# Block 0's convolution with two product buffers, a split of its last taps between GpSimd and VectorE, and carried rows loaded in pieces

## The chip, the cores and the metric

The program runs on one core of one Trainium2 chip. The engines that matter are TensorE (PE in the rows; PEld is its weight load), VectorE (DVE), ScalarE (ACT), GpSimd (POOL), and SyncE (SP), whose queue issues the transfers. The metric is the device time of one execution in microseconds; less is better. A kernel's time is the median of several executions.

## What is computed

A dynamic convolution over 7 positions, with softmax weights, feeds two fully connected pairs.

```python
B, S, D = 2, 4096, 192            # H, K = 8 heads, 7 taps; group = D // H = 24
w = exp(weight_gen - max(weight_gen, axis=-1)); w = w / (sum(w, axis=-1) + 1e-09)
x_pad = concatenate([zeros((B, K - 1, D)), x], axis=1)
out[b, s, h, :] = sum over k of w[b, s, h, k] * x_pad[b, s + k, h, :]
x = out.reshape(B * S, D)                                    # 8192 tokens
h = x @ moe_w_in                                             # 192 -> 2048
x = where(h >= 1, h, where(h <= -1, 0, (h + 1) ** 2 / 4)) @ moe_w_out
h = x @ moe2_w_in
return (h - tanh(h)) @ moe2_w_out                            # 8192 x 192, float32
```

## The kernel before

**Tiling.** Each of the 128 partitions holds 64 consecutive tokens of one sequence. The 8192 tokens are worked in 16 blocks `b` of 512, four tokens (`T`) of every partition. A block passes its convolution (`conv`), its first pair (`m = 0`) and its second pair (`m = 1`). A pair takes 16 items of 128 hidden columns: five matmuls into a bank (`mm1`, L540), the activation (L546 to L548, or L550 and L551), a split of the result into a rounded part `gh` (L552) and a rest `gl` (L556), and the second matmuls (L564 to L571, or L581 to L584).

**Weights.** Both pairs' weights arrive as 64-bit words in chunks (`weights`): ScalarE and VectorE join the halves (L305, L310, L314, L319), ScalarE casts the high part (L337), and VectorE or GpSimd makes the low part (L341). All 32 chunks are prepared in the first 180 us or so.

**The convolution of an early block (0 and 1).** `load_wg` (L375) brings the softmax weights' inputs, `load_halo` the carried rows: the first taps of a partition's first tokens need up to six rows of the partition before it, `w[lo+1:hi, 0:n0]`, 63 partitions for each of the two sequences, in two transfers (L386); the one partition without a neighbour is set to zero by GpSimd (L385). `load_x` (L378) brings the rest. The softmax is L406 to L416; its result `wg` is copied to PSUM (L427), so that VectorE can read it there. VectorE multiplies four taps (L419), each into the one product area `prod_ps` in PSUM, and adds each to `acc` (L461). GpSimd multiplies the other three into `taps`, in SBUF, and adds them up (L445). `last_sum` adds the two partial sums in two pieces, L468 to `acc` and L470 into `xw`; both inputs are in SBUF. Then TensorE transposes (L478, L481), and ScalarE and VectorE split the result (L498 to L510) for the first `mm1`.

**The order of the work.** `Plan` builds each engine's order ahead of time: every task has an engine or a choice of engines, a duration, a key and the slots that it takes. `run` steps through time and gives a free engine its ready task of lowest key. For VectorE it models a lock: a task marked `lock` waits while GpSimd works, and its key grows by that wait. Chunk weights with the lowest key go ahead of convolution steps with a higher one; block 0's convolution has keys from -60, block 1's from `CONV1`. The transfers are issued from SP's queue in the planned order, and wait there for their buffers.

Of the kernel before, what the change touches and what calls it, by code (L numbers as in the profile page):

```python
# [17 lines left out]
P = 128  # L18
N = 512
T = N // P  # L20
LAG = 3
RAW = 4
EARLY = 2
POOL_TAPS = (3, 3)
REBIAS = 2.0 ** -112
ITEM = 2.275

# [19 lines left out]
class Plan:  # L47
# [20 lines left out]
    def run(self):  # L68
# [17 lines left out]
        while events:  # L86
# [10 lines left out]
            for e in ready:  # L97
                if free[e] > now + 1e-9:
                    continue
                kept, got = [], None  # L100
                pool_busy = max(0.0, free.get("POOL", 0.0) - now) if e == "DVE" else 0.0
                if pool_busy:

                    ready[e] = [(t.key + t.engines[e][1] + (pool_busy / ITEM if t.lock else 0.0), t.order, t) for _, _, t in ready[e] if t.start is None]
                    heapq.heapify(ready[e])
                while ready[e]:
                    c = heapq.heappop(ready[e])
                    t = c[2]
                    if t.start is not None:
                        continue  # L110
                    pick, ok = [], True
                    for s in t.takes:
                        n = s.choice()
                        if n is None:
                            ok = False
                            break
                        s.free.remove(n)
                        pick.append((s, n))
                    if ok:
                        for s, n in pick:  # L120
                            s.n = n
                        got = t
                        break
                    for s, n in reversed(pick):
                        s.free.insert(0, n)
                    kept.append(c)
                for c in kept:
                    heapq.heappush(ready[e], c)
                if got is None:
                    continue  # L130
                t, dur = got, got.engines[e][0]
                if e == "DVE" and t.lock:
                    dur += pool_busy
                    free["POOL"] = max(free.get("POOL", 0.0), now + dur)
                    locked = now + dur
                elif e == "POOL" and locked > now:
                    dur += locked - now
                t.start, t.engine, t.took = now, e, dur
                t.seen = now + dur + t.late
                free[e] = now + dur  # L140
                heapq.heappush(events, now + dur)
                heapq.heappush(events, t.seen)
                done.append(t)
                for s in t.uses:
                    s.users -= 1
                    if s.users == 0:
                        heapq.heappush(returns, (t.seen, t.order, id(s), s))
                for d in t.next:
                    d.blocked -= 1
                    if d.blocked == 0:  # L150
                        when = max(q.seen - (q.late - q.own if q.engine in d.engines else 0.0) for q in d.deps)
                        heapq.heappush(waiting, (when, d.order, d))
                        heapq.heappush(events, when)
# [9 lines left out]
def tile_dynconv_moe_moe(  # L163
# [43 lines left out]
    make_identity(nc, ident)  # L207
    half = const.tile([P, 1], F32, tag="half", name="half")
    nc.vector.memset(half, 0.5)

    nc.scalar.activation(const.tile([P, 1], F32, tag="warm", name="warm"), half, AF.Exp)


    win = tiles("win", 2, [P, 4, FF], F32R)
    wout = tiles("wout", 2, [P, NF, 2 * D], F32R)
# [144 lines left out]
    def conv(b, banks, base, gap):  # L360
# [15 lines left out]

        def load_x(e):
            e.dma_start(xws[xw.n][:, n0:, :], x_pj[:, j0 - PAD + n0:j0 + T, :])  # L378

        def load_halo(e):  # L380

            w = xws[xw.n]
            for q in range(B):
                lo, hi = q * BP, (q + 1) * BP
                nc.gpsimd.memset(w[lo:lo + 1, 0:n0, :], 0.0)  # L385
                e.dma_start(w[lo + 1:hi, 0:n0, :], x_pj[lo:hi - 1, J - n0:J, :])  # L386

        def bc(t):
            return t.unsqueeze(3).to_broadcast([P, T, H, K])
# [35 lines left out]

        if early:
            tw = plan.add(on("ACT", 0.30), key(), lambda e: e.copy(wg_ps, W()), [ts], uses=[wg] + area)  # L427
            mine = K - POOL_TAPS[b]
            prod, wsrc = prod_ps, lambda: wg_ps
            dep = [tw]  # L430

            def pool_mem(k):
                return xt_t[spare.n][:, k]

            pt = [ts, lx, lh]
            first = True
            for k in range(mine, K):
                def ptap(e, k=k, first=first):
                    if first:
                        xt_tile(spare, f"taps{b}", (P, 2, T, D), F32)  # L440
                    tap(e, pool_mem(0 if first else 1), W(), k)

                pt = [plan.add(on("POOL", 1.6), base, ptap, pt, takes=[spare] if first else [], uses=[wg, xw] + ([] if first else [spare]), late=0.1)]
                if not first:
                    pt = [plan.add(on("POOL", 1.6), base, lambda e: e.tensor_tensor(pool_mem(0), pool_mem(0), pool_mem(1), op=ALU.add), pt, uses=[spare], late=0.1)]  # L445
                first = False
            addend = lambda: pool_mem(0)
        else:
            mine = K
            prod, wsrc = prod_sb, W  # L450
            dep, pt = [ts], []
            addend = lambda: prod_sb
        more = (area if early else [])
        for k in range(mine):
            def mult(e, k=k):
                tap(e, prod if k else acc_sb, wsrc(), k)

            t = plan.add(on("DVE", 0.87), key(), mult, dep + [whole(k), lh], takes=[] if k else [mem], uses=[wg, xw] + more + ([mem] if k else []), late=0.1, own=0.12 if early and k else 0.0, lock=not early)
            dep = [t]
            if k and (k < mine - 1 or early):  # L460
                t = plan.add(on("DVE", 0.87), key(), lambda e: e.tensor_tensor(acc_sb, acc_sb, prod, op=ALU.add), dep, uses=[mem] + more, late=0.1, lock=not early)  # L461
                dep = [t]

        flat = lambda: xws[xw.n].rearrange("p j d -> p (j d)")[:, 0:T * D1]

        def last_sum(e):
            s = addend()
            e.tensor_tensor(acc_sb[:, :, 0:P], acc_sb[:, :, 0:P], s[:, :, 0:P], op=ALU.add)  # L468

            e.tensor_tensor(flat().rearrange("p (t c) -> p t c", t=T), acc_sb[:, :, P:D], s[:, :, P:D], op=ALU.add)  # L470

        t = plan.add(on("DVE", 0.97), key(), last_sum, dep + pt, uses=[mem, xw] + more + ([spare] if early else []), lock=True)

        p0, p1 = ps[banks[0]], ps[banks[1]]

        def transposes(e):
# [6 lines left out]
        last = key()  # L483
        tr = plan.add(
            on("PE", 0.70), last, transposes, [t, marks.get(("fin1", 0 if b == 2 else b - 1)) if b == 2 or b > 3 else None],
            takes=[] if early else area, uses=[mem, xw] + more, late=0.4,
        )
        X = lambda k: xt_t[xt.n][:, k]

# [166 lines left out]
UNTIL = 3.5  # L656
SKEW = 12
LEAD = (4.0, 6.0)
CONV1 = (4.0, 0.35)
CONV2 = (14.0, 0.6)  # L660


# [27 lines left out]
```

## Time and profile before

| | us |
|---|---|
| median of 3 runs (1232.03 to 1232.91) | 1232.22 |
| the profiled execution | 1232.54 |
| its span, first to last instruction | 1230.7 |
| TensorE busy in the span | 1193.1 |
| VectorE busy | 984.5 |
| ScalarE busy | 831.5 |
| GpSimd busy | 100.2 |

The profiled execution has 1.84 us around its span. A row of the timeline is one instruction or some alike: start, duration, engine, line, operation, names, and in brackets how long the engine had been idle and what ended that. Two instructions of VectorE that depend on each other follow with a small gap; two that don't may overlap by a little.

### The profile page before, as it was taken

What the parts mean: (1) busy time and instruction counts of PE and PEld (TensorE: products, weight loads), DVE (VectorE), ACT (ScalarE), POOL (GpSimd) and SP (SyncE); (2) the same over time, 40 slices, a digit from 0 to 9 for tenths busy, and PEclk for the clock granted to TensorE, in tenths of its full rate; (3) what the DMA queues carried; (4) which work ended last, traced back from release to release, by engine and by line L of the source; (5) the groups of instructions that cost most, each with busy time, mean ns of one, the idle gap of its engine ahead of it and who ended that gap; (6) DMA issues with size and microseconds to landing.
All of it is one profiled execution on the core that took longest, in us unless ns stands there. A gap on an engine that the chain in (4) does not pass through costs nothing.

```text
span 1230.7 us, 16226 instructions
## 1 busy us (share of the span) xinstructions
PE 1193.1 (97%) x5984; PEld 1024.9 (83%) x5984; DVE 984.5 (80%) x1535; ACT 831.5 (68%) x1500; POOL 100.2 (8%) x84
## 2 busy tenths in 40 slices
PE   3799999999999999999999999999999999999998
PEld 2577879889888898988889888888988889888897
DVE  7999988868779697886968779696887968676665
ACT  5888985675766657576675766667576675766654
POOL 5644560000000000000000000000000000000000
PEclk9899999999999999999999999999999999999999
DMA  8422221001000010100101000010100000000000
GB/s 218 141 88 67 72 77 45 18 1 32 18 32 18 1 36 14 33 17 4 46 1 33 18 32 17 1 37 14 33 17 18 29 1 1 13 1 14 1 14 13
DMA packets 16494, 39.55 MB, mean 32 GB/s; under 512 B 1828, under 2 KB 8098, under 8 KB 16416
## 3 DMA queue, kind: packets, MB, share of 16 engines
q1 hardware_dynamic: 16416, 38.53, 9.9%
q8 instruction: 46, 0.75, 0.3%
q14 instruction: 32, 0.26, 0.1%
HBM read 32.23 MB, written 6.29 MB: 31 GB/s over the span
## 4 chain that ended last, share of the span: by engine, by line
PE 85%; DVE 0%; DVEq 0%; issue 0%
PE ps L540 43%; PE ps L581 14%; PE ps L582 7%; PE ps L565 4%; PE ps L564 4%; PE ps L566 4%; PE ps L571 4%; PE ps L570 4%; PE ps L584 1%; PE ps L478 0%; PE ps L481 0%; DVE raw L618 0%; DVE ps L314 0%; DVE g L551 0%; DVEq L686 0%
## 5 line engine op out<-in xcount | busy, mean ns | idle before, releaser
L556 DVE TENSOR_TENSOR gl<-g,gh 128x512 fp32r<-128x512 f32 x475 | 329.6, 696 | 184.8 <-ACT gh L552 182.1
L552 ACT CAST gh<-g 128x512 fp32r<-128x512 f32 x512 | 315.6, 617 | 202.9 <-DVE g L551 182.5
L540 PE MATMUL ps<-a,win 128*128 128x512 f32 x1280 | 340.8, 397 | 8.2 <-DVE g L548 6.9
L540 PE MATMUL ps<-b,win 128*128 128x512 f32 x1280 | 339.2, 395 | 1.5 <-DVE g L548 0.7
L540 PEld LDWEIGHTS ps<-a,win 128*128 128x128 f32 x1280 | 239.4, 191 | 63.2 <-DVE g L548 13.2
L581 PE MATMUL ps<-wout,gh 128*128 128x384 f32 x960 | 286.1, 354 | 0.0
L540 PEld LDWEIGHTS ps<-b,win 128*128 128x128 f32 x1280 | 225.3, 188 | 40.3 <-DVE g L551 2.1
L582 PE MATMUL ps<-wout,gl 128*128 128x192 f32 x1024 | 256.7, 251 | 0.4 <-POOL gl L556 0.3
L546 ACT ACTIVATE g<-ps 128x512 f32<-128x512 f32 x256 | 152.4, 595 | 108.0 <-PE ps L540 104.9
L582 PEld LDWEIGHTS ps<-wout,gl 128*128 128x128 f32 x1024 | 194.8, 190 | 10.1 <-POOL gl L556 0.6
L551 DVE TENSOR_TENSOR g<-ps,g 128x512 f32<-128x512 f32 x256 | 175.7, 687 | 27.1 <-ACT g L550 26.6
L581 PEld LDWEIGHTS ps<-wout,gh 128*128 128x128 f32 x960 | 180.2, 188 | 9.4
L550 ACT ACTIVATE g<-ps 128x512 f32<-128x512 f32 x256 | 152.5, 596 | 49.7 <-PE ps L540 47.5
L548 DVE SCALAR_TENSOR_TENSOR g<-ps,g 128x512 f32<-128x512 f32 x256 | 173.8, 683 | 7.0 <-ACT g L547 6.6
L547 ACT ACTIVATE g<-g 128x512 f32<-128x512 f32 x256 | 162.4, 634 | 3.2
L570 PE MATMUL ps<-gl,wout 128*128 128x512 f32 x256 | 100.3, 392 | 0.8 <-POOL gl L556 0.7
L564 PE MATMUL ps<-gh,wout 128*128 128x512 f32 x256 | 100.4, 392 | 0.0
L565 PE MATMUL ps<-gh,wout 128*128 128x512 f32 x256 | 100.2, 391 | 0.0
L566 PE MATMUL ps<-gh,wout 128*128 128x512 f32 x256 | 100.1, 391 | 0.0
L571 PE MATMUL ps<-gl,wout 128*128 128x512 f32 x256 | 99.6, 389 | 0.0
L419 DVE TENSOR_TENSOR prod<-xw,wg 128x768 f32<-128x768 f32 x84 | 82.2, 979 | 0.0
L461 DVE TENSOR_TENSOR acc<-acc,prod 128x768 f32<-128x768 f32 x70 | 69.3, 990 | 0.4
(67 smaller groups left out, 742.3 us busy)
## 6 DMA issues: line engine op xcount, KB each, us to landing
xw<-in_x_dram SPq DMA_DIRECT2D x14, 960.0 KB, 4.8
raw<-in_moe_w_out_dram SPq DMA_DIRECT2D x16, 384.0 KB, 3.3
out_dram<-raw SPq DMA_DIRECT2D x16, 384.0 KB, 2.3
raw<-in_moe_w_in_dram SPq DMA_DIRECT2D x16, 256.0 KB, 3.4
raw<-in_moe_w_in_dram SPq DMA_DIRECT2D x32, 128.0 KB, 3.6
wg<-in_weight_gen_dram SPq DMA_DIRECT2D x16, 112.0 KB, 2.0
xw<-in_x_dram SPq DMA_DIRECT2D x1, 768.0 KB, 6.1
xw<-in_x_dram SPq DMA_DIRECT2D x2, 283.5 KB
```

Source lines behind the costliest of these rows:

```text
L540: e.matmul(ps[h.n], w[:, k, fs], xt[:, c], start=n == 0, stop=n == len(ops) - 1)
L546: t = plan.add(on("ACT", 0.60), i, lambda e: e.activation(G_(), H_(), AF.Relu, bias=0.5, scale=0.5), [first], takes=[g], uses=[h], late=0.1)
L547: t = plan.add(on("ACT", 0.537), i, lambda e: e.activation(G_(), G_(), AF.Square), [t], uses=[g])
L548: t = plan.add(on("DVE", 0.605), i, lambda e: e.scalar_tensor_tensor(G_(), H_(), 1.0, G_(), op0=ALU.max, op1=ALU.min), [t], uses=[g, h])
L550: t = plan.add(on("ACT", 0.49), i, lambda e: e.activation(G_(), H_(), AF.Tanh), [first], takes=[g], uses=[h])
L551: t = plan.add(on("DVE", 0.605), i, lambda e: e.tensor_tensor(G_(), H_(), G_(), op=ALU.subtract), [t], uses=[g, h])
L552: thi = plan.add(on("ACT", 0.527), i, lambda e: e.copy(GH(), G_()), [t], takes=[gh], uses=[g])
L556: tlo = plan.add(engines, i, lambda e: e.tensor_tensor(GL(), G_(), GH().bitcast(F32), op=ALU.subtract), [thi], takes=[gl], uses=[g], lock= ...
L564: e.matmul(p0, w[:, 0:P], GH(), start=a, stop=False)
L570: e.matmul(p1, w[:, 2 * P:], GL(), start=False, stop=z)
L581: e.matmul(q[n][:, 0:2 * D], GH()[:, ts], w, start=a, stop=False)
L582: e.matmul(q[n][:, 0:D], GL()[:, ts], w[:, 0:D], start=False, stop=False)
```

## The change

Six things are altered:

- `load_halo`: each sequence's 63 partitions are loaded in two transfers, of 48 and of 15 partitions; those of the second sequence are issued from ScalarE's queue. The zeros are set by VectorE.
- The warm-up activation, which loads ScalarE's table, is issued behind block 0's loads.
- Block 0 takes a second PSUM pair, banks 4 and 5, as a second product buffer. Its four taps and three sums on VectorE are put in the order tap, tap, tap, sum, tap, sum, sum, and the last sum is left in PSUM.
- GpSimd adds only the first two of its three taps. VectorE adds that sum in one more instruction (L488 of the new kernel), then the third tap in `last_sum`, whose first operand is now in PSUM. Block 1 has the same with one product buffer.
- In the planner: GpSimd's tasks of the convolution have a key lower by 3; VectorE's queue is keyed anew at each step, not only while GpSimd is busy.
- Block 1's convolution starts from key 0 instead of 4.

```diff
-POOL_TAPS = (3, 3)
...
-                if pool_busy:
+                if e == "DVE":
...
-    nc.scalar.activation(const.tile([P, 1], F32, tag="warm", name="warm"), half, AF.Exp)
...
         def load_x(e):
             e.dma_start(xws[xw.n][:, n0:, :], x_pj[:, j0 - PAD + n0:j0 + T, :])
+            if b == 0:
+
+                nc.scalar.activation(const.tile([P, 1], F32, tag="warm", name="warm"), half, AF.Exp)
...
-            for q in range(B):
+            for q, queue in zip(range(B), (e, nc.scalar)):
                 lo, hi = q * BP, (q + 1) * BP
-                nc.gpsimd.memset(w[lo:lo + 1, 0:n0, :], 0.0)
-                e.dma_start(w[lo + 1:hi, 0:n0, :], x_pj[lo:hi - 1, J - n0:J, :])
+                cut = lo + 1 + (BP - 1) // 16 * 16
+                for a, z in ((lo + 1, cut), (cut, hi)):
+                    queue.dma_start(w[a:z, 0:n0, :], x_pj[a - 1:z - 1, J - n0:J, :])
+                nc.vector.memset(w[lo:lo + 1, 0:n0, :], 0.0)
...
+            area2 = bank(4, 5) if b == 0 else area
+            prods = [prod_ps, pairs[4][:, 0:T * D].rearrange("p (j d) -> p j d", d=D) if b == 0 else prod_ps]
...
+            pk = base - 3.0
+            t = plan.add(on("POOL", 1.55), pk, lambda e: ptap(e, 0, K - 3), [ts, lx, lh], takes=[spare], uses=[wg, xw], late=0.1)
+            t = plan.add(on("POOL", 1.55), pk, lambda e: ptap(e, 1, K - 2), [t], uses=[wg, xw, spare], late=0.1)
+            pa = plan.add(on("POOL", 1.65), pk, padd, [t], uses=[spare], late=0.1)
+            pb = plan.add(on("POOL", 1.55), pk, lambda e: ptap(e, 1, K - 1), [pa], uses=[wg, xw, spare], late=0.1)
...
+            def add(e, k=k):
+
+                e.tensor_tensor(prods[k % 2] if early and k == mine - 1 else acc_sb, acc_sb, prods[k % 2], op=ALU.add)
...
+        if b == 0:
+            tasks = [tasks[n] for n in (0, 1, 3, 2, 5, 4, 6)]
...
+        end = prods[(mine - 1) % 2]
+        if early:
+            dep = [plan.add(on("DVE", 0.87), key(), lambda e: e.tensor_tensor(end, end, pool_mem(0), op=ALU.add), dep + [pa], uses=more + [spare], own=0.12)]
+
         def last_sum(e):
...
+            u, v = (end, pool_mem(1)) if early else (acc_sb, prod_sb)
+            e.tensor_tensor(acc_sb[:, :, 0:P], u[:, :, 0:P], v[:, :, 0:P], op=ALU.add)
+
+            e.tensor_tensor(flat().rearrange("p (t c) -> p t c", t=T), u[:, :, P:D], v[:, :, P:D], op=ALU.add)
...
-CONV1 = (4.0, 0.35)
+CONV1 = (0.0, 0.35)
```

On VectorE, block 0's taps and sums stand like this before; `acc`, `ps_61` and `taps_128` are the sum, the product area and GpSimd's part, `raw`, `val` and `win` are the weights' chunks:

```order
L419 TENSOR_TENSOR ps_61<-xw_88,ps_61 128x768
L314 SCALAR_TENSOR_TENSOR ps_63<-ps_63,raw_80 128x512
L461 TENSOR_TENSOR acc_94<-acc_94,ps_61 128x768
L319 SCALAR_TENSOR_TENSOR val_84<-raw_80,ps_63 128x512
L314 SCALAR_TENSOR_TENSOR ps_64<-ps_64,raw_81 128x512
L319 SCALAR_TENSOR_TENSOR val_85<-raw_81,ps_64 128x512
L341 TENSOR_TENSOR win_76<-val_84,win_76 128x2x256
L468 TENSOR_TENSOR acc_94<-acc_94,taps_128 128x4x128
L470 TENSOR_TENSOR xw_88<-acc_94,taps_128 128x256
```

The same engine and place now (`ps_61` and `ps_62` are the two product buffers, L488 is the added sum, L492 and L494 are the last sum):

```order
L421 TENSOR_TENSOR acc_92<-xw_86,ps_61 128x768
L421 TENSOR_TENSOR ps_62<-xw_86,ps_61 128x768
L421 TENSOR_TENSOR ps_61<-xw_86,ps_61 128x768
L468 TENSOR_TENSOR acc_92<-acc_92,ps_62 128x768
L421 TENSOR_TENSOR ps_62<-xw_86,ps_61 128x768
L388 MEMSET xw_87 1x384 x2
L468 TENSOR_TENSOR acc_92<-acc_92,ps_61 128x768
L468 TENSOR_TENSOR ps_62<-acc_92,ps_62 128x768
L488 TENSOR_TENSOR ps_62<-ps_62,taps_130 128x768
L310 SCALAR_TENSOR_TENSOR ps_63<-ps_63,raw_78 128x512
L492 TENSOR_TENSOR acc_92<-ps_62,taps_130 128x4x128
L494 TENSOR_TENSOR xw_86<-ps_62,taps_130 128x256
```

Before, five weight instructions stand between the taps and the last sum; now one (L310), with the two zeroings of block 1's rows and the added sum.

GpSimd before, from the start of its taps (`win` and `wout` are low parts of weights, `gl` the rest of an item):

```order
L419 TENSOR_TENSOR taps_128<-xw_88,wg_86 128x768 x2
L445 TENSOR_TENSOR taps_128<-taps_128 128x768
L419 TENSOR_TENSOR taps_128<-xw_88,wg_86 128x768
L445 TENSOR_TENSOR taps_128<-taps_128 128x768
L341 TENSOR_TENSOR win_76<-val_85,win_76 128x2x256
L385 MEMSET xw_89 1x384 x2
```

GpSimd now, from the same place:

```order
L421 TENSOR_TENSOR taps_130<-xw_86,wg_84 128x768 x2
L447 TENSOR_TENSOR taps_130<-taps_130 128x768
L421 TENSOR_TENSOR taps_130<-xw_86,wg_84 128x768
L337 TENSOR_TENSOR win_74<-val_82,win_74 128x2x256
L337 TENSOR_TENSOR win_74<-val_83,win_74 128x2x256
L421 TENSOR_TENSOR taps_212<-xw_87,wg_85 128x768 x2
```

One sum and the zeroings are gone, both first chunks' low parts are GpSimd's, and block 1's taps come directly behind them. Over the whole program VectorE's instructions on low parts go from 9 to 4 of `win` (128x2x256), from 2 to 3 pairs of `wout` (128x2x128 with 128x2x64), and from none to 3 of `wout` of the second pair (128x2x192); those on `gl` go from 475 to 474. TensorE's order is the same for all but some first 470 of its 3874 rows, VectorE's for all but some first 420 of its 1520.

## Rows read from the trace of the kernel before

**Rows 1.** The page: span, and each engine's busy time, share and instructions.

```profile
span 1230.7 us, 16226 instructions
PE 1193.1 (97%) x5984; PEld 1024.9 (83%) x5984; DVE 984.5 (80%) x1535; ACT 831.5 (68%) x1500; POOL 100.2 (8%) x84
```

**Rows 2.** Busy time by stretch: length, engines with counts, granted clock, DMA share, GB/s.

```profile
0.00:20.00 20.00, 0.22 (x1) 0.25 (x2) 14.46 (x22) 7.81 (x14) 13.19 (x16) 1.00 0.81 199
...
40.00:70.00 30.00, 24.48 (x88) 17.98 (x86) 28.71 (x48) 25.36 (x54) 19.97 (x17) 0.83 0.48 145
...
180.00:1230.00 1050.00, 1045.82 (x5372) 911.56 (x5372) 820.41 (x1290) 683.26 (x1212) 3.80 (x4) 1.00 0.05 18
```

**Rows 3.** Waits from 20 to 180 us: waiter, releaser, total us, times, longest.

```profile
PE ps L478 <- DVE acc L468: 21.9, 2, 19.8
...
PEld ps L540 <- DVE g L548: 14.3, 16, 3.7
...
DVE g L548 <- ACT g L547: 3.0, 4, 1.0
```

**Rows 4.** TensorE's waits from 180 us to the end.

```profile
PE ps L540 <- DVE g L551: 0.6, 1, 0.6
```

**Rows 5.** The timeline of the first 20 us: start, duration, instruction, idle before.

```profile
0.74 0.38 SPq L375 DMA_DIRECT2D wg<-in_weight_gen_dram  x1
...
0.88 1.05 POOL L385 MEMSET xw<- 1x1152 f32 x1
1.18 0.70 SPq L386 DMA_DIRECT2D xw<-in_x_dram  x2
...
2.93 0.39 DVE L406 TENSOR_REDUCE ps<-wg 128x32 f32<-128x224 f32 x1 [2.05 <-DMA wg<-in_weight_gen_dram]
...
5.68 0.35 ACT L427 COPY ps<-wg 128x224 f32<-128x224 f32 x1 [1.51 <-DVE wg L416]
...
7.51 0.95 DVE L419 TENSOR_TENSOR acc<-xw,ps 128x768 f32<-128x768 f32 x1 [1.87 <-DMA xw<-in_x_dram]
8.50 0.96 DVE L419 TENSOR_TENSOR ps<-xw,ps 128x768 f32<-128x768 f32 x1
...
8.94 3.04 POOL L419 TENSOR_TENSOR taps<-xw,wg 128x768 f32<-128x768 f32 x2 [5.57 <-DMA xw<-in_x_dram]
...
15.58 1.82 POOL L445 TENSOR_TENSOR taps<-taps 128x768 f32<-128x768 f32 x1
...
17.61 1.47 POOL L341 TENSOR_TENSOR win<-val,win 128x512 fp32r<-128x512 f32 x1 [0.22 <-ACT win L337]
...
17.87 1.76 DVE L468 TENSOR_TENSOR acc<-acc,taps 128x512 f32<-128x512 f32 x1
...
19.55 0.41 DVE L470 TENSOR_TENSOR xw<-acc,taps 128x256 f32<-128x256 f32 x1
...
19.78 1.09 PE L478 MATMUL ps<-ident,acc 128*128 128x128 f32 x4 [19.78 <-DVE acc L468]
```

**Rows 6.** Busy time by short stretches of the first 9 us, columns as in rows 2.

```profile
2.50:3.50 1.00, 0.00 (x0) 0.00 (x0) 0.54 (x2) 0.00 (x0) 0.87 (x1) 1.00 0.47 139
...
4.50:7.50 3.00, 0.00 (x0) 0.00 (x0) 1.04 (x4) 0.35 (x1) 0.00 (x0) 1.00 1.00 241
```

**Rows 7.** VectorE's groups to 180 us by shape: count, busy us, mean ns, idle before.

```profile
L556 DVE TENSOR_TENSOR gl<-g,gh 128x512 fp32r<-128x512 f32 x19 | 16.4, 870 | 0.1
...
L341 DVE TENSOR_TENSOR win<-val,win 128x512 fp32r<-128x512 f32 x9 | 8.6, 957 | 0.0
...
L319 DVE SCALAR_TENSOR_TENSOR val<-raw,ps 128x384 uint32<-128x384 uint32 x14 | 7.6, 541 | 0.0
...
L341 DVE TENSOR_TENSOR wout<-val,wout 128x256 fp32r<-128x256 f32 x2 | 2.0, 984 | 0.1
L341 DVE TENSOR_TENSOR wout<-val,wout 128x128 fp32r<-128x128 f32 x2 | 1.9, 953 | 0.0
```

**Rows 8.** The last sum of later blocks, to 180 us: duration ns min/median/max.

```profile
L468 DVE TENSOR_TENSOR acc<-acc,prod x2: 714/1223/1732, 99.9 to 157.8; 128x512 f32<-128x512 f32 x2
```

## What was predicted

> **What bounds the kernel now.** I read the busy times first: TensorE is busy for 97% of the span [rows 1]. The stretches say where the rest is: from 180 us on it is busy for 1045.82 of 1050 us, and it then waits 0.6 us for another engine [rows 2, 4]. So the end of the program is the end of the front part plus a fixed remainder, and a microsecond saved before 180 us is saved at the end. What the front part is bound by, the stretches and waits show. Up to 19.78 us TensorE does nothing: it waits for the last sum of block 0's convolution [rows 3, 5]. From 40 to 70 us VectorE is busy for 28.71 of 30 us and TensorE for 24.48 at a mean granted clock of 0.83 [rows 2], and the longest repeated wait of the stretch up to 180 us is TensorE's for VectorE's activation, 14.3 us in 16 waits [rows 3]. The front part thus has two accounts: a chain, up to the first transposes at 19.78 us, and VectorE's total work, which fills nearly all of the time behind it. Only the smaller of the two gains reaches the end.
>
> **Part 1, the start of the taps.** The first tap starts at 7.51 us, 1.87 us after VectorE became free; the softmax's copy had ended at 5.68 + 0.35 = 6.03, so it is the carried rows that were late [rows 5]. The rows were issued at 1.18 us, and up to 3.5 us the transfer engines were busy for a share of 0.47 [rows 6]: 0.58 MB (126 rows of 1152 values) went through about half of them. With 48 and 15 partitions the pieces can fill all. At the 241 GB/s of the full stretch [rows 6] 0.58 MB need 2.4 us; with the weights' inputs of 0.11 MB ahead of them and a start near 2 us they land at about 5 us, at the latest (half again as long) near 6.2. The softmax then sets the start. Its first instruction began at 2.93 and the copy ended at 6.03, with 0.04 to the tap 3.14 us later. What can delay it is new: VectorE now zeroes two rows of 1152 first. GpSimd took 1.05 us for one [rows 5]; two from 0.87 us on end at 2.97. And the second queue's rows are issued at the same moment as the softmax's inputs and compete with them: 0.22 MB at 241 GB/s are 0.9 us, so the inputs land between 2.9 and 3.8. I take 3.4, thus a first tap at 6.55; bounds 6.1 and 7.4, a gain of 0.96, from 0.1 to 1.4. ScalarE's two issues and the table load (issues of 0.35 us by SP's pair of 0.70 [rows 5]) end before the exponential needs ScalarE.
>
> The Trainium skill speaks both ways here. "DMA: Bandwidth & Descriptors", section "Why a DMA increments its semaphore by 16 and not by 1", says that a transfer is spread over the largest number of engines up to 16 that divides its slowest dimension: 9 for 63 partitions, 16 and 15 for the pieces; the share of 0.47 agrees. Its section "Issuing engines are not separate DMA queues" says that a second queue saves only issue time; by that alone nothing of the 0.96 would come, and the sum below would be 2.4.
>
> **Part 2, from the first tap to the transposes.** Before, the first tap and the last sum are 17.87 - 7.51 = 10.36 us apart [rows 5]. Now the order has, between them, eight wide instructions (four taps, three sums, the added sum), two zeroings of 384 and one weight join. A dependent wide instruction follows after 0.99 us (7.51 to 8.50). One that need not wait overlaps its predecessor by 0.08, as L470 does, which starts at 19.55 while L468 ends at 17.87 + 1.76 = 19.63 [rows 5]; so it follows after 0.87. Of the eight four are followed at once: 4 x 0.87 + 4 x 0.99 = 7.44. That is all that the second buffer gives, 4 x 0.12 = 0.5. The zeroings are a third of 1152 each: two, about 0.75. The join is 0.72 with its gap (a 384-wide one takes 0.54 [rows 7], this is 512). Sum 8.91. The last sum itself took 1.76 because GpSimd was at work on weights from 17.61 [rows 5]; one with both inputs in SBUF and nothing in its way took 0.71 [rows 8], and with one input in PSUM I take 0.71 here. So the last sum ends at 6.55 + 8.91 + 0.71 = 16.17, instead of 19.63: the transposes come **3.5 us** earlier. GpSimd does not undo that: it started its taps at 8.94, when the rest of the rows had landed [rows 5]; even from there 3.04 for two taps and 1.82 for the sum [rows 5] end at 13.8, before the added sum (6.55 + 7.2 = 13.8), and the third tap at 15.4, before the last sum at 15.46. With the transfer engines filled earlier it starts near 7.
>
> But four weight instructions, 3.3 us, were only moved behind the last sum, not removed. VectorE must still do them, so the second account has to be made.
>
> **Part 3, VectorE's account up to 180 us.** Removed or shortened: the wait for the rows 0.96; the overlaps 0.5; both last sums of blocks 0 and 1, 2 x (1.76 - 0.71) = 2.1; five `win` parts that go to GpSimd, 5 x 0.957 = 4.8; one `gl`, 0.87 [rows 7]. Added: two wide sums, 2 x 0.98 = 2.0; the zeroings of block 1, 0.75; one more pair of `wout`, 0.98 + 0.95 = 1.9 by its row, 0.54 by the row of as many columns without a hindrance [rows 7]; three second-pair `wout` of 128x384, 3 x 0.6 = 1.8. Balance: 9.2 - 6.45 = **2.8**, or 4.2 with the cheaper pair. If the five `win` parts are worth only their shortest time of about 0.7, it is 1.5.
>
> The two accounts meet near 3.5. I take 3.4 us. Whatever else in the order differs ends up in the same place: the orders agree beyond the first few hundred instructions, and no wait of TensorE was left there to be filled [rows 4].
>
> **Part 4, block 1 pulled forward.** Its taps and sums now stand ahead of the activations of block 0's items: up to the fifth activation VectorE has some seven wide instructions more and five parts of weights or `gl` fewer ahead of it, 7 x 0.95 less 5 x 0.68 and the rest, about 4 us. Up to the 13th it has five parts and four joins fewer, 3 us less than before. So TensorE waits earlier and less later; in between nothing is lost as long as VectorE does not idle. I cost it at nothing; the cover is that VectorE is the bound there.
>
> **Rivals.**
>
> *Better: the idling goes too.* VectorE waited 3.0 us for ScalarE's squares [rows 3], part of it in the first items after 22 us, while TensorE had just begun. If the first items come in a tighter order, and the moved `win` parts save the full 1.05 that most of them took, 2 to 3 us more are won: span gain near 6, **1226.2**. For it: ready work (block 1's softmax) now fills those gaps. Against: the waits of ScalarE and VectorE on each other belong to every item.
>
> *Nothing: the hindrance moves.* The gains of 2.1 at the last sums and of the 0.27 above the shortest in each `win` part are times in which VectorE was held up by GpSimd. GpSimd's work is nearly as long as before, so other two-input instructions of VectorE may be held up instead. Then the account is 4.2 - 2.1 - 5 x 0.27 = 0.8 or less: **1231.6**. If the rows' landing gains nothing either, it is zero.
>
> *Slower: GpSimd's five more weight parts hold VectorE up.* Each lasts 1.47 us [rows 5] and stands beside VectorE's wide sums and casts of block 1 and 2. If each holds up one of them for 1.05, as L468 was, that is 5.25; the three second-pair parts, if held up as the first pair's (0.95 instead of 0.54 [rows 7]), 1.2 more. -3.4 + 5.25 + 1.2 = +3.1: **1235.3**. It decides once the hold-ups up to 180 us grow by more than 3.4 + 2.5 = 5.9 us. Against it: the new sums have an input in PSUM.
>
> *Not what it says.* If the rows do not land sooner, because pieces from two queues slow each other and the softmax's inputs, the first tap stays near 7.5 and both accounts lose 0.96: 2.4 us, **1229.8**. Against it is the share of 0.47 [rows 6], which leaves room for more at once. The Trainium skill's sentence on issuing engines, above, is this rival's rule.
>
> **How the numbers follow.** Profiled span 1230.7, less 3.4, is 1227.3; with the 1.84 outside it 1229.1. The profiled execution was 0.32 above the median of the runs, so 1228.8 against 1232.22. A measurement here tells about 0.2%, 2.46 us, from no change: the border is 1229.8. The forecast, from 1227.3 to 1230.3, has 0.37; the better case 0.20; the rows gaining nothing 0.10; nothing at all 0.18; slower 0.15. The range leaves out the slower case and a small part of the better one: 1225.0 to 1232.6. Faster by over 0.2%: most of the forecast, half of the case on the rows, and the better case, 0.30 + 0.05 + 0.20 = 0.55. Within: the rest of these and nothing at all, 0.12 + 0.18 = 0.30. Slower: 0.15.
>
> **What would show it right or wrong.** Right: a first tap between 6.1 and 7.0, no wait for `xw` ahead of it, transposes near 16.3, L492 near 0.7 us, GpSimd done with block 0's taps before 15 us, and TensorE's last wait near 176.5 us. The step on the rows is wrong if the tap still waits for them; the one on the second queue if the softmax starts after 3.8. The accounts are wrong if the transposes are 3 us early but TensorE's last wait is not: then VectorE's groups up to 180 us show which part grew. The forecast falls if VectorE's means for `prod` and `acc` of blocks 2 and 3 rise, or if ScalarE becomes the one waited for.

## The result, and the profile after

The changed kernel takes 1246.62 us (median of 4 runs, 1245.77 to 1246.94) against 1232.12 us before (4 runs beside them): a ratio of 1.0118, 95% interval 1.0105 to 1.0130. It is **slower by 14.5 us**; 1228.8 was forecast, and the range ended at 1232.6. The profiled execution took 1246.94 us, its span 1245.2.

The busy times of the page come first. TensorE executes as many instructions as before and is busy 14.7 us longer [rows 1]; no other engine grew by as much:

```profile
span 1245.2 us, 16241 instructions
PE 1207.8 (97%) x5984; PEld 1024.5 (82%) x5984; DVE 989.2 (79%) x1540; ACT 832.4 (67%) x1500; POOL 98.3 (8%) x79
```

TensorE by stretch (length, busy us, matmuls, granted clock, share and GB/s of the transfers), first before, then after; a granted clock of 1.00 is TensorE's upper level, 2.4 GHz:

```profile
0.00:180.00 180.00, 147.25 (x613) 0.97 0.39 113
...
200.00:1200.00 1000.00, 1000.00 (x5112) 1.00 0.06 19
```

```profile
0.00:180.00 180.00, 147.71 (x614) 1.00 0.38 113
...
200.00:1200.00 1000.00, 1000.00 (x5033) 1.00 0.05 18
```

These rows find the loss. At 180 us both kernels have done the same amount, 613 and 614 matmuls: the loss is not in the front part. From 200 to 1200 us TensorE is busy in every microsecond of both, at full granted clock, with the same order of instructions; but it gets through 79 matmuls fewer. So each one takes longer. Which ones, its groups by shape show, from 400 to 1100 us (busy us, mean ns of one; the duration reaches past the start of the next matmul), before:

```profile
L540 PE MATMUL ps<-b,win 128*128 128x512 f32 x775 | 205.4, 395 | 0.0
L540 PE MATMUL ps<-a,win 128*128 128x512 f32 x750 | 195.5, 390 | 0.0
L581 PE MATMUL ps<-wout,gh 128*128 128x384 f32 x568 | 169.6, 355 | 0.0
...
L565 PE MATMUL ps<-gh,wout 128*128 128x512 f32 x153 | 59.6, 389 | 0.0
```

and after:

```profile
L564 PE MATMUL ps<-a,win 128*128 128x512 f32 x755 | 200.5, 396 | 0.0
L564 PE MATMUL ps<-b,win 128*128 128x512 f32 x745 | 199.6, 398 | 0.0
L605 PE MATMUL ps<-wout,gh 128*128 128x384 f32 x548 | 163.8, 355 | 0.0
...
L589 PE MATMUL ps<-gh,wout 128*128 128x512 f32 x155 | 61.2, 395 | 0.0
```

The matmuls of 512 columns are 3 to 6 ns longer, those of 384 are not. From start to start, successive ones of `gh` went from 227.0 to 232.4 ns, of `a` from 228.7 to 233.5, and of `b` from 234.2 to 236.5. There are 3840 of 512 columns in the program: at 3 to 6 ns that is 11.5 to 23 us, and the 14.7 us lie in it.

The first 20 us after show what became of the front part (columns as in rows 5):

```profile
0.73 1.12 ACTq L387 DMA_DIRECT2D xw<-in_x_dram  x2
...
0.73 0.39 SPq L371 DMA_DIRECT2D wg<-in_weight_gen_dram  x1
...
1.06 1.02 DVE L388 MEMSET xw<- 1x1152 f32 x1 [0.20 <-issue]
1.18 0.93 SPq L387 DMA_DIRECT2D xw<-in_x_dram  x2
...
2.36 1.02 DVE L388 MEMSET xw<- 1x1152 f32 x1 [0.28 <-issue]
...
5.50 0.40 DVE L408 TENSOR_REDUCE ps<-wg 128x32 f32<-128x224 f32 x1 [2.12 <-DMA wg<-in_weight_gen_dram]
...
8.30 3.04 POOL L421 TENSOR_TENSOR taps<-xw,wg 128x768 f32<-128x768 f32 x2 [7.00 <-DVE wg L418]
8.63 0.95 DVE L421 TENSOR_TENSOR acc<-xw,ps 128x768 f32<-128x768 f32 x1 [0.41 <-ACT ps L429]
...
16.31 0.97 DVE L488 TENSOR_TENSOR ps<-ps,taps 128x768 f32<-128x768 f32 x1
...
17.78 0.68 DVE L492 TENSOR_TENSOR acc<-ps,taps 128x512 f32<-128x512 f32 x1
...
18.61 1.09 PE L502 MATMUL ps<-ident,acc 128*128 128x128 f32 x4 [18.61 <-DVE acc L492]
```

The softmax starts at 5.50 us instead of 2.93 [rows 5]: VectorE had been idle for 2.12 us, until the weights' inputs `wg` landed. The first tap follows at 8.63 instead of 7.51, and the transposes come at 18.61, 1.2 us earlier than before and not 3.5.

### The profile page after: what moved, and what is told of

Read it like the earlier page. It is cut to its first block, busy times and chain, and to the rows that moved or that the text cites. A ratio compares the mean times of both kernels' runs of the same rounds, so it can differ in the third digit from the quotient of the medians.

```text
span 1245.2 us, 16241 instructions
## 1 busy us (share of the span) xinstructions
PE 1207.8 (97%) x5984; PEld 1024.5 (82%) x5984; DVE 989.2 (79%) x1540; ACT 832.4 (67%) x1500; POOL 98.3 (8%) x79
## 4 chain that ended last, share of the span: by engine, by line
PE 88%; DVE 6%; ACT 3%; issue 2%; POOL 1%; DMA 0%; DVEq 0%; ACTq 0%
PE ps L564 44%; PE ps L605 14%; PE ps L606 7%; PE ps L594 4%; PE ps L595 4%; PE ps L588 4%; PE ps L589 4%; PE ps L590 4%; DVE gl L580 1%; PE ps L608 1%; DVE g L572 1%; ACT gh L576 1%; ACT g L570 1%; DVE prod L421 1%; DVE acc L468 1%
## 5 line engine op out<-in xcount | busy, mean ns | idle before, releaser
L580 DVE TENSOR_TENSOR gl<-g,gh 128x512 fp32r<-128x512 f32 x474 | 333.5, 706 | 195.4 <-ACT gh L576 187.8
L564 PE MATMUL ps<-a,win 128*128 128x512 f32 x1280 | 346.0, 401 | 11.1 <-DVE g L572 10.0
L594 PE MATMUL ps<-gl,wout 128*128 128x512 f32 x256 | 101.9, 398 | 2.0 <-POOL gl L580 1.2
L595 PE MATMUL ps<-gl,wout 128*128 128x512 f32 x256 | 101.2, 395 | 0.0
```

The costliest lines, as they stand in the source:

```text
L564: e.matmul(ps[h.n], w[:, k, fs], xt[:, c], start=n == 0, stop=n == len(ops) - 1)
L580: tlo = plan.add(engines, i, lambda e: e.tensor_tensor(GL(), G_(), GH().bitcast(F32), op=ALU.subtract), [thi], takes=[gl], uses=[g], lock= ...
L594: e.matmul(p1, w[:, 2 * P:], GL(), start=False, stop=z)
```

## The experiments

Two things were to be explained: why matmuls that the change doesn't touch became slower, and why the softmax's inputs came late.

### The warm-up's 32 bytes

The diff moves one statement that has an effect besides its time: it allocates `warm`, which takes 32 bytes of every partition for its one number. Before, that stood ahead of the weights' tiles; now it runs in `load_x`, when all of them have their places. So in the built program everything from `win` to `gl` lies 32 bytes lower (`win0` at 17056 instead of 17088, `gh0` at 182176 instead of 182208), while `a` and `b` lie where they lay. The theory: the placement makes the matmuls slower. The rival: something in the order of the work does. The first run puts `warm` back in its old place and leaves the instruction in its new one:

```diff
+    warm = const.tile([P, 1], F32, tag="warm", name="warm")
     win = tiles("win", 2, [P, 4, FF], F32R)
...
-                nc.scalar.activation(const.tile([P, 1], F32, tag="warm", name="warm"), half, AF.Exp)
+                nc.scalar.activation(warm, half, AF.Exp)
```

> The changed kernel, but the 128x1 tile that the warm-up writes is allocated where it was before, ahead of the weights' tiles, so that all tiles of weights, activations and their splits lie at the same SBUF addresses as in the kernel before (32 bytes further than in the changed kernel); the order of the instructions is that of the changed kernel. Theory A (the addresses: a 32-byte shift slows TensorE's 512-column matmuls from 227 to about 232 ns): 1232.5 us, within 2 us of the kernel before, intervals of 227 ns again. Theory B (the new order of the front part leaves TensorE slower for the rest, by its clock or by the rhythm of the buffers): 1246.5 us, intervals near 232 ns.

It took 1231.51 us, ratio to before 0.9995 [0.9986, 1.0004]. TensorE is back at its old pace:

```profile
0.00:180.00 180.00, 147.67 (x618) 1.00 0.37 113
200.00:1200.00 1000.00, 1000.00 (x5112) 1.00 0.06 19
```

The next run does the reverse: the kernel before, with nothing but its warm-up statement moved below the tiles.

```diff
-    nc.scalar.activation(const.tile([P, 1], F32, tag="warm", name="warm"), half, AF.Exp)
     win = tiles("win", 2, [P, 4, FF], F32R)
...
     gl_t = tiles("gl", LAG + 1, [P, N], F32R)
+    nc.scalar.activation(const.tile([P, 1], F32, tag="warm", name="warm"), half, AF.Exp)
```

> The kernel before, with the warm-up's tile allocated behind the splits' tiles: every tile from the weights to the splits lies 32 bytes lower, as in the changed kernel; the instructions and their order are those of the kernel before. Theory A: 1246 us (14 us slower), 512-column matmuls near 232 ns apart. Theory B: 1232.2 us, no change.

1246.14 us, ratio 1.0120 [1.0103, 1.0137], with 5033 matmuls from 200 to 1200 us, as in the changed kernel. So the whole loss comes with the placement of one tile, **shown in both directions**.

### Which placement is slow

Four runs shift groups of tiles of the kernel before. Only the weights `win` and `wout` lie 32 bytes lower, with `warm` allocated ahead of `WC`:

> The kernel before, with only the four weight tiles (win, wout) 32 bytes lower, at 32 modulo 64; all others as before. If the slow operand is the weights of the first and the moved side of the second pair's second matmul: mm1 (L540) slower by about 4 ns of each of 2560, so about +10 us, and the second matmuls of the first pair unchanged or slower by their stationary operand. If the slow operand is the split activations (gh, gl): 1232.2 us. Theory B: 1232.2 us.

1249.28 us, ratio 1.0142 [1.0127, 1.0158]. Next, with `half` ahead of `g` and `warm` behind `gl`, `g`, `gh` and `gl` come to lie 32 bytes lower, the weights 64:

> The kernel before, with only the activations and their splits (g, gh, gl) at 32 modulo 64; the weights at a multiple of 64. If the slow operand is gh or gl: the first pair's second matmuls (L564 to L571) slower by about 5 ns of each of 1280, +6 us, mm1 (L540) unchanged or slowed by other engines' use of these tiles. If it is the weights: 1232.2 us. Theory B: 1232.2 us.

1241.84 us, ratio 1.0081 [1.0066, 1.0097]. With both behind `gl`, all from `win` to `gl` lie 64 bytes lower, and every tile is at a multiple of 64 again:

> The kernel before, with all tiles from the weights to the splits 64 bytes lower (two 32-byte tiles moved behind them), while the tiles a and b stay: the distance between the two groups changes by 64, and every start is still a multiple of 64. If the remainder modulo 64 decides: 1232.2 us, matmuls 227 ns apart. If any change of the distance or of the place does it: 1240 us or more.

1241.31 us, ratio 1.0091 [1.0075, 1.0107]. A multiple of 64 is thus not what counts. With 32 unused bytes behind `gl`, only `a` and `b` move, 32 bytes up:

```diff
     gl_t = tiles("gl", LAG + 1, [P, N], F32R)
+    tiles("pad0", 1, [P, 8])
```

> The kernel before, with only the convolution's and first pair's results (a, b: the moved side of mm1) at 32 modulo 64. If every operand of TensorE at 32 modulo 64 costs: mm1 (L540) 4 to 8 ns slower in each of 2560, +10 to +20 us, second matmuls unchanged. If only weights, gh and gl count: 1232.2 us.

1245.88 us, ratio 1.0126 [1.0112, 1.0141]. That is the same as 32 bytes down for all the others, which speaks for the distance between tiles and against their addresses. The decisive run has the same pad ahead of `win`: then every tile that TensorE reads is 32 bytes higher, and no distance has changed but that to the unit matrix of the transposes.

> The kernel before with 32 unused bytes ahead of the first weight tile: the weights, the items' tiles and the transposed inputs a and b all lie 32 bytes higher, so no distance among the operands of TensorE changes, only their addresses. Theory of the distance (the interval of a 512-column matmul depends on how the tiles that are read together lie to each other): 227 ns between starts as before, and 1232 us, within 2. Theory of the address (each tile has to lie at a multiple of 64 bytes): 232 to 235 ns, and 1246 us, within 4.

1231.17 us, ratio 0.9994 [0.9985, 1.0003]. TensorE's rows, first with `a` and `b` alone shifted, then with all:

```profile
200.00:1200.00 1000.00, 1000.00 (x5032) 1.00 0.05 18
```

```profile
200.00:1200.00 1000.00, 1000.00 (x5115) 1.00 0.06 19
```

**It is the distance.** Between what, a program of its own tells, run once: 14 stretches of 100 matmuls of 512 columns, in which the stationary tile is shifted by `wa` values of 4 bytes and the moving one by `xb`. In short:

```python
for n in range(100):
    a, b = wa + 128 * (n % 7), xb + 512 * (n % 2)
    nc.tensor.matmul(ps[n // 5 % 2], w[:, a:a + 128], xt[:, b:b + 512], start=n % 5 == 0, stop=n % 5 == 4)
```

> Fourteen stretches of 100 matmuls of 512 columns with nothing else in the program: in eight only TensorE works, with the stationary tile and the moving tile shifted by 0, 16, 32, 64 or 128 bytes, singly and together; in six ScalarE copies each finished bank and VectorE adds to the copy beside it. Leaves out the whole computation of the reference. If TensorE's own two reads hinder each other, the stretches of TensorE alone with one of the two shifted by 32 bytes take 232 to 235 ns from start to start instead of 227, and those with both shifted 227. If the hindrance comes from the other engines' reads and writes, all eight alone take 227 ns, and only stretches with ScalarE and VectorE beside them take more. If neither shows more than 227 ns, the cause lies in something that this program doesn't have, the change between kinds of matmul among it.

TensorE in stretches of 22 us; the shifts of `wa` and `xb` are in this order 0 and 0, 0 and 32 bytes, 0 and 64, 0 and 128, both 32; then, with ScalarE and VectorE at work on the results, 0 and 32:

```profile
32.00:54.00 22.00, 22.00 (x99) 1.00 0.00 0
55.00:77.00 22.00, 22.00 (x96) 1.00 0.00 0
78.00:100.00 22.00, 22.00 (x98) 1.00 0.00 1
101.00:123.00 22.00, 22.00 (x96) 1.00 0.00 1
...
147.00:169.00 22.00, 22.00 (x99) 1.00 0.00 0
...
216.00:238.00 22.00, 22.00 (x96) 1.00 0.00 1
```

From start to start these are 226.7, 233.3, 228.9, 232.4, 226.7 and 233.3 ns; 32 bytes on the stationary tile alone give 233.3 too, 16 bytes on the moving one 231.7. No other engine works in the first five of these rows, and adding two changes nothing. So it is TensorE's own two tiles that matter, and in these stretches only their distance counts. The second such program, also run once, moves `xb` further:

> Fourteen stretches of 100 matmuls of 512 columns with TensorE alone, as in the micro_offsets run, now with the moving tile alone shifted, by 0, 0, 96, 160, 192, 224, 256, 288, 320, 384, 448, 512, 768 and 1024 bytes. Leaves out the whole computation of the reference. There, 0 took 227 ns between starts, 16 bytes 231.7, 32 bytes 233.4, 64 bytes 229.0 and 128 bytes 232.3. In the kernel before, the weights and the transposed inputs lie a multiple of 256 bytes apart, but not of 512, and mostly take 227 ns. Theory (the distance counts modulo 256 bytes or less): 256, 512, 768 and 1024 bytes take 227 ns, and all others 229 to 235. Rival (only distance modulo 512 counts, or only zero is good): 256 and 768 bytes take 229 to 235 as well.

Shifts of 224, 256, 288 and 768 bytes, in stretches of 21 us:

```profile
124.00:145.00 21.00, 21.00 (x92) 1.00 0.00 1
148.00:169.00 21.00, 21.00 (x94) 1.00 0.00 0
171.00:192.00 21.00, 21.00 (x92) 1.00 0.00 1
...
286.00:307.00 21.00, 21.00 (x94) 1.00 0.00 1
```

256, 512, 768 and 1024 bytes take 227 ns, as no shift does; 96, 160, 192, 224, 288, 384 and 448 bytes take 232 to 234, and 320 takes 229, like 64. **In the distances tried, the pattern repeats every 256 bytes.** In the kernel before, the weights, the items' tiles and `a` and `b` all start at 192 past a multiple of 256; in the changed one two of the three are at 160.

The Trainium skill says otherwise of the engine's ports. "TensorE: Matmul & The Clock Gate", section "Step-by-step: what each phase is for", states that the loading of the next weights takes no read bandwidth from the running matmul, the two having ports of their own. The stretches differ from it: with TensorE alone, the distance of its two operands costs up to 7 ns in 227. Which of the two reads waits, they don't show. "SBUF — State Buffer", section "Who interferes with whom", states that TensorE never waits on anyone, which is said of the other engines; with that the stretches agree, 233.3 ns with ScalarE and VectorE beside it and without.

Two runs shift one operand alone, `win1`, which only the matmuls of `b` read. It is allocated ahead of `win0`, and so comes to lie 32 or 64 bytes lower modulo 256, while `win0` keeps its remainder. They start from the best kernel below (1228.64 us).

> The sp_pool_block1_late kernel (1228.6 us) with the second pair's first weights (win1) alone 32 bytes lower. In the kernel before, its matmuls of b and win1 take 234 ns between starts, against 227 to 229 for those of the first pair. Theory of single pairs of operands: only the matmuls of b and win1 change, those of a and win0 and of gh, gl and wout keep their means within 1 ns; by the 600 such matmuls the time moves by no more than 600 x 7 ns = 4.2 us either way, 1224.4 to 1231. Theory that matmuls hand the delay on (each starts its own reads earlier or later by what came before it): those of gh and gl change by over 1 ns too, although no address of theirs has changed.

1232.15 us, ratio to before 1.0002 [0.9993, 1.0012]. Successive matmuls of `b` went from 234.2 to 237.0 ns, and the last one of `gl` ahead of a `b` from 226.7 to 235; those of `a`, `gh` and `gl` among themselves stayed within 0.5. In this run the loss thus stays with the matmuls of `b` and their neighbours. That of `gl` ahead of a `b` reads only tiles that did not move; what moved are the weights of the matmul behind it. The 3.5 us lost are more than the 2.4 that the bound left upwards: it counted 600 matmuls of `b`, about those between 400 and 1100 us, where the program has 1280; 1280 x 2.8 ns are 3.6 us.

> The same with win1 64 bytes lower. By the micro_offsets run, a distance of 64 bytes off takes 229 ns where 32 bytes takes 233: if the 234 ns of b and win1 in the kernel before have to do with the distance, they come nearer to 229 here, 1225.5 us (600 x 5 ns less); if not, 1228.6 or, with a delay handed on to the others, up to 1234.

1232.14 us, ratio 1.0003 [0.9993, 1.0012]. The matmuls of `b` took 235.1 ns instead of the 229 hoped for. This mean hides two kinds, which the trace of the kernel before shows: five matmuls of `b` behind the second pair's matmuls of 192 columns (1.18 us to the next start), and five behind one of 512 (1.14 us).

```profile
500.67 0.25 PE L582 MATMUL ps<-wout,gl 128*128 128x192 f32 x1
500.76 1.34 PE L540 MATMUL ps<-b,win 128*128 128x512 f32 x5
501.94 0.34 PE L581 MATMUL ps<-wout,gh 128*128 128x384 f32 x1
...
560.47 0.39 PE L571 MATMUL ps<-gl,wout 128*128 128x512 f32 x1
560.69 1.30 PE L540 MATMUL ps<-b,win 128*128 128x512 f32 x5
561.83 0.39 PE L564 MATMUL ps<-gh,wout 128*128 128x512 f32 x1
```

Behind one of 512 (of `gl`), successive matmuls of `b` take 226.7 ns from 400 to 1100 us, as those of `a` there do; behind one of 192, the first of five takes 253 and the next three 230 to 233, with `b` as with `a`. So the 234 ns have nothing to do with `win1`: `b` more often stands behind 192 columns. Among the five behind one of 512, `win1` 32 bytes lower gives 233.3 ns and 64 lower 228.9, the figures of the program with TensorE alone (233.3 and 228.9).

Those of `gh` and `gl` took about 1 ns more with `win1` 64 bytes lower (`gh` 227.0 to 228.0), though none of their addresses had changed. In the run that moved `a` and `b` alone, successive matmuls of `gh` had gone from 227.0 to 232.4 ns in the same way, so a theory of single pairs alone doesn't hold. Both agree with a delay that is handed on; they don't prove it.

### The second queue, the zeros and block 1

With the placement mended, the other parts can be measured. First all pieces of the carried rows from SP's queue:

```diff
-            for q, queue in zip(range(B), (e, nc.scalar)):
+            for q, queue in zip(range(B), (e, e)):
```

> The changed kernel with the warm-up's tile at its old place (addresses as before), and all four pieces of carried rows issued from SP's queue, behind the softmax's inputs; nothing else changed. Theory C (the second queue's rows compete with the softmax's inputs, which landed at 5.5 us instead of 2.9): the inputs land by 3.0 us, the first tap starts at 6.5 us (the zeroings end at 3.4) instead of 8.6, the transposes near 16.5 instead of 18. If the chain up to the transposes reaches the end: 1229.3 us, 2 us less than with two queues. Rival D (VectorE's total work or the order up to 180 us sets the end): 1231 to 1232 us, however early the transposes are.

1229.83 us, ratio 0.9987 [0.9978, 0.9996]. Its timeline:

```profile
3.31 0.32 DVE L409 TENSOR_REDUCE ps<-wg 128x32 f32<-128x224 f32 x1
...
6.59 0.95 DVE L422 TENSOR_TENSOR acc<-xw,ps 128x768 f32<-128x768 f32 x1 [0.63 <-DMA xw<-in_x_dram]
...
15.74 0.68 DVE L493 TENSOR_TENSOR acc<-ps,taps 128x512 f32<-128x512 f32 x1
...
16.57 1.08 PE L503 MATMUL ps<-ident,acc 128*128 128x128 f32 x4 [16.57 <-DVE acc L493]
```

The softmax starts 2.2 us earlier than in the changed kernel, directly behind VectorE's zeroing, and the first tap is at 6.59 us, where 6.55 was forecast. At the first tap the second queue thus cost 2.0 us, 8.63 - 6.59, more than the pieces gain over the kernel before, 7.51 - 6.59 = 0.9. Next, the zeros go back to GpSimd:

```diff
-                nc.vector.memset(w[lo:lo + 1, 0:n0, :], 0.0)
+                nc.gpsimd.memset(w[lo:lo + 1, 0:n0, :], 0.0)
```

> As the run before (all rows from SP, addresses as before), with the zeroings on GpSimd again. Theory C: the softmax starts at 2.9, the first tap at 6.1 or when the rows land, 0.4 us before the other run's; VectorE has 0.9 us less to do. If the chain reaches the end: 1228.9 us. Rival D: 0.9 us less than the run before by VectorE's work, or nothing.

1229.03 us, ratio 0.9986 [0.9977, 0.9995]. The softmax starts at 2.83, but the first tap again waits for the rows, now for 1.36 us instead of 0.63, and comes 0.3 us later than in the run above, not 0.4 earlier:

```profile
2.83 0.40 DVE L409 TENSOR_REDUCE ps<-wg 128x32 f32<-128x224 f32 x1 [1.95 <-DMA wg<-in_weight_gen_dram]
...
6.91 0.95 DVE L422 TENSOR_TENSOR acc<-xw,ps 128x768 f32<-128x768 f32 x1 [1.36 <-DMA xw<-in_x_dram]
...
15.88 1.09 PE L503 MATMUL ps<-ident,acc 128*128 128x128 f32 x4 [15.88 <-DVE acc L493]
```

Last, block 1's convolution from key 4, as before (`CONV1 = (4.0, 0.35)`):

> The changed kernel with its weights at the addresses of the kernel before, all carried rows from one queue and the zeros set by GpSimd (1229.0 us), and block 1's convolution starting from key 4 again, as before. My theory (Part 4: the forward shift moves waits, and is worth nothing at the end): within 1.5 us of 1229.0, with TensorE earlier than there at the 40th matmul and later at the 120th. Rival (the forward shift carries part of the gain, or costs some): 1231 or more, or 1227 or less.

1228.64 us, ratio 0.9973 [0.9963, 0.9982], the fastest kernel of the study, ahead of both that were given. It differs from the run above by 0.4 us, and from the 680th matmul on TensorE differs by 0.2 us: the forward shift is worth nothing at the end. At the 40th matmul TensorE is 3.6 us earlier, as expected; at the 120th it was expected later and is 0.8 us earlier, and at the 160th it is 1.0 us later.

## Why the prediction was wrong

**The fixed remainder** is the step that failed. "The end of the program is the end of the front part plus a fixed remainder" was read from rows that are right: TensorE waits 0.6 us in all after 180 us [rows 4], and 0.9 us in the changed kernel. But a stretch without waits is fixed only if its instructions keep their durations, and those of the 512-column matmuls went, for `gh`, from 227.0 to 232.4 ns, which cost 15.1 us in all (1246.62 against 1231.51 with the old placement). The diff had the cause in plain sight, the tile allocated inside the moved warm-up statement; I costed that statement as an instruction of ScalarE, and not as an allocation. Of the rivals none had a place after 180 us. The slower one, GpSimd's hold-ups at 1235.3, gave the right sign for another reason than the one that made it slower.

**Part 1, the first tap.** Forecast 6.55, at most 7.4; it came at 8.63, outside the bounds. The mis-sized term is the landing of the softmax's inputs, taken at 3.4 us with an upper bound of 3.8, measured 5.50. The bound counted 0.22 MB of competing bytes at 241 GB/s; with ScalarE's two transfers issued from the same moment on (0.73 us) the inputs took 4.8 us from their issue. From one queue they took 2.1, and 2.6 at most where VectorE's zeroing stood ahead of the softmax. The transfers' packets show where the time went: the last one of the inputs ended at 4.46 us, when 0.28 MB of the second queue's 0.29 had been moved, and at 2.43 and 2.46 us with one queue. The text had named this sign beforehand: a softmax after 3.8 us. That the pieces fill the transfer engines held: from 2.5 to 3.5 us their share is 0.88 and 0.91 in the two runs with one queue, instead of 0.47 [rows 6]. The carried rows' landing was too hopeful all the same: about 5 us, at the latest 6.2, was forecast, and where the softmax doesn't hide them they let the tap start at 6.59 and 6.91. The Trainium skill's rule, "DMA: Bandwidth & Descriptors", section "Issuing engines are not separate DMA queues", that a second queue saves issue time only, was the better guide to the second queue: nothing came of it here. It has no figure for inputs that come 2.6 us later.

**Part 2, from the first tap to the transposes.** Right. From the first tap to the last sum 8.91 us were forecast, and it took 17.78 - 8.63 = 9.15; the last sum took 0.68 for 0.71 forecast. GpSimd was done with its third tap at 14.86, before 15. With one queue the transposes come at 16.57 and 15.88, about the forecast 16.17 to 16.3.

**Part 3, VectorE's account.** Its sum came near, for partly other reasons, and how much of the gain is its own is not shown. VectorE's groups of the first 180 us after (columns as in rows 7):

```profile
L580 DVE TENSOR_TENSOR gl<-g,gh 128x512 fp32r<-128x512 f32 x18 | 19.7, 1097 | 1.3 <-ACT gh L576 1.3
L421 DVE TENSOR_TENSOR prod<-xw,wg 128x768 f32<-128x768 f32 x12 | 12.7, 1062 | 0.0
L468 DVE TENSOR_TENSOR acc<-acc,prod 128x768 f32<-128x768 f32 x10 | 10.0, 996 | 0.0
...
L337 DVE TENSOR_TENSOR win<-val,win 128x512 fp32r<-128x512 f32 x4 | 3.9, 977 | 0.4 <-ACT win L333 0.2
...
L492 DVE TENSOR_TENSOR acc<-ps,taps 128x512 f32<-128x512 f32 x2 | 1.4, 680 | 0.0
```

The `win` parts saved 8.6 - 3.9 = 4.7 of the forecast 4.8 us [rows 7], and the two last sums 2.2 of 2.1. But a `gl` took 1097 ns instead of 870 [rows 7], 18 x 0.227 = 4.1 us more. That is the mechanism of the rival "the hindrance moves": the sums got free of GpSimd, and the items' rests met it; all eight `gl` of over 1 us overlap work of GpSimd in the trace. In exchange VectorE's waits for ScalarE's squares fell from 3.0 us [rows 3] to 0.6, which the better case had named. With the placement and the queue mended, TensorE has done 625 to 631 matmuls at 180 us instead of 613, and the time is by the medians 2.4 to 3.5 us under before, where the two accounts had given 3.4. In the kernel with two queues it is 0.6, which the interval doesn't tell from nothing.

Nor is all of this shown to be VectorE's account, because the kernel before varies with TensorE's clock. Beside the first two of these runs, 8 of its executions had a mean granted clock of 0.998 and a median of 1230.05 us, 12 had 0.996 or 0.997 and 1232.34. Against the former the gains are 0.2 and 1.0 us. Beside the last of them, the fastest, five executions at 0.998 took 1231.10, which leaves 2.5. That the gain came near the 3.4 of the accounts may thus be luck.

**Part 4, block 1.** Right: nothing at the end.

So of the 14.5 us lost, the placement is 1246.62 - 1231.51 = 15.1; the rest of the change, as given, gains 0.6 by the medians, and without the second queue 2.4, with what was said of the clock.

## What to carry to other kernels

A diff is also a change of the memory map: where a statement that allocates is moved, added or dropped, compare the addresses of all operands before calling the rest of the program fixed. Keep the tiles that TensorE reads together a multiple of 256 bytes apart, as these 512-column matmuls of float32r wanted it, and pad small tiles that lie between them. A second queue for a large transfer is no gain when a small one that the chain waits for is issued in the same moment: issue the small one first, and the large ones behind it.

## What was not expected of the hardware

- 32 bytes of distance between the two operands of a 512-column matmul cost 3% of its time (226.7 to 233.3 ns), with no other engine at work. The second pair's matmuls of 384 and 192 columns kept their 355 and 251 ns in the changed kernel, but there the distance of their own operands had not changed. From start to start, one of each together took 278.9 ns before and 279.6 in the changed kernel, but 281.6 with the weights alone 32 bytes lower and 282.2 in the run with `gh` and `gl` 32 and the weights 64 bytes lower: about 1%.
- Behind a matmul of 192 columns, the first of five of 512 takes 253 ns to the next start instead of 226.7, whichever weights it uses. Why is open, and so is how a matmul hands a delay on to others whose addresses are unchanged.
- The granted clock between 40 and 70 us, 0.83 before [rows 2], was 1.00 in the changed kernel. Before, it was at the lower level (1.2 GHz) from 45.8 to 52.7 us and from 59.5 to 62.9; in the 5.0 us ahead of the first fall TensorE had been busy for 2.97, in the 6.8 ahead of the second for 4.57. In the changed kernel it was busy for 26.93 of these 30 us instead of 24.48, at 2.4 GHz. No experiment changed the clock alone; executions of the kernel before at a mean of 0.998 or more took 0.9 to 2.3 us less than those below it, in the medians of four rounds.
